# A limit on the loads in flight at the start of a fused attention and expert kernel

## The chip, the core and the metric

The kernel runs on one core of one Trainium2 chip. The metric is the device time of one execution in microseconds (us); the number that counts is the median of the runs. The profile adds one execution recorded in detail, whose span runs from the first to the last instruction.

## The reference

Three stages follow each other. What is computed, cut to what matters (the masks are a plain window of 32 positions for heads 0 to 3, and a window of 128 in steps of 4 for heads 4 to 7):

```python
# q, k, v: [2, 8, 576, 64]
scores = where(mask, q @ k.T / sqrt(64), -1e9)
attn   = softmax(scores);  x = attn @ v             # reshaped to [1152, 512]
h      = x @ w_in                                   # w_in [512, 1024], float64
solu   = h * softmax(h)
ln     = (solu - mean) / sqrt(var + 1e-6) * g_ln
x2     = ln @ w_out                                 # w_out [1024, 512], float64
for e in range(4):                                  # w1 [4, 512, 1024], w2 [4, 1024, 512]
    out += p[:, e] * (relu(x2 @ w1[e]) @ w2[e])
```

## The kernel before

Everything is written out by hand: `ORDER` (L31 to L53) is a list of steps, and each engine gets its instructions in that order. Each step takes one piece of a generator. The steps with a lower-case `l` are loads, all issued by SyncE (SP, its queue is shown as SPq) and all on one hardware queue, in the order of the list: `lP`/`lD` fetch a tile of q and k (416 or 448 KB, `load_qk`, L151), `lvp`/`lvd` a tile of v (384 KB, L159 and L154), `lI` a block of 128 rows of `w_in` (`load_in`, L203 to L212) and `lO` one of `w_out` (512 KB, `load_out`, L228). `lI.0` and `lI.4` are the two halves of block 0 of `w_in`, 512 KB each; `lI.1`, `lI.2` and `lI.3` are whole blocks of 1 MB.

SP issues 28 loads of this kind in the first 31 us, and one of 22 KB (`misc`). Their order begins

1 `lP.0.0`, 2 `lI.4`, 3 `lD.0.0`, 4 `lD.1.0`, 5 `lP.1.0`, 6 `lI.0`, 7 `lP.2.0`, 8 `lD.2.0`, 9 `lI.1`, 10 `lI.2`, 11 `lvp.0.0`, 12 `lvd.1.0`, 13 `lI.3`, 14 `lvp.1.0`, 15 `lvd.0.0`, 16 `lD.1.1`, 17 and 18 `lO.0.0` and `lO.0.1`, then `misc` and ten more tiles of q, k and v.

These numbers are used below. The program has eight completion semaphores for its DMAs and gives them out in turn, so an issue also waits until the load that had its semaphore before, eight DMAs back, has landed.

What the loads feed: `UP`/`UD` (`att_U`, L257) is one unit of attention, with the score matmuls at L275 (q and k needed), maximum, subtraction, exponent and sum on VectorE (DVE, L296 to L305) and ScalarE (ACT, L301), and the product with v at L337. `VI` (`conv_in`, L214) turns a block of float64 `w_in` into two float32r parts: ACT L190 and L192 read the raw block (`draw`), DVE L194, L196 and L198 put the bits together, L223 and L225 split the result. `conv_in` works on a whole block of 1 MB at once for blocks 1 to 3, and on a half for block 0. `H` (`moe_H`, L367) is x @ w_in on TensorE (PE); `F` is a matmul on a constant tile, without use for the result. After the front come the expert products at L562 and L634.

Of the kernel before, what the change touches and what calls it, by code (L numbers as in the profile page):

```python
# [13 lines left out]
I64 = mybir.dt.int64  # L14
# [9 lines left out]
SWAP = (3, 4, 5, 6, 7, 8)  # L24
ROWS = (5,)
EB = 4
VB = 3
EXPB = ()
ASWAP = ("UD.0.1", "UD.1.1", "UD.2.1", "UP.1.1", "UP.2.1")
# [26 lines left out]
def fused_kernel(ctx, tc, qkp, qkd, vp, vd, w_in, w_out, gp, w1, w2, out):  # L56
    nc = tc.nc
# [44 lines left out]
    xlo = wp.tile([128, KD, NT], F32R, name="xlo", tag="xlo")  # L102
    ep = lnw.enter_context(tc.tile_pool(name="ep", bufs=EB))
    cvs = ExitStack()
# [3 lines left out]
    ap2 = at.enter_context(tc.tile_pool(name="ap2", bufs=2))  # L108
    ap3 = at.enter_context(tc.tile_pool(name="ap3", bufs=VB))
    early = ExitStack()  # L110
    erp = early.enter_context(tc.tile_pool(name="erp", bufs=1, side="right"))

    qkP, qkD, vdt = [], [], []
# [31 lines left out]
    nc.gpsimd.memset(mhalf, -0.5)  # L145

    vps = {}

    def load_qk(quad, t, b):
        dst, src = ((qkD, qkd), (qkP, qkp))[quad == "P"]  # L150
        nc.sync.dma_start(out=dst[b][t], in_=src[b, t])  # L151

    def load_vd(c, b):
        nc.sync.dma_start(out=vdt[b][c].rearrange("p m h d -> p (m h d)"), in_=vd[b, c])  # L154

    def load_vp(u, b):
        t = ap3.tile([128, 3, 4, D], F32, name="vp", tag="vp")
        vps[u, b] = t
        nc.sync.dma_start(out=t.rearrange("p m h d -> p (m h d)"), in_=vp[b, u])  # L159

    whi, wlo = {}, {}
    alt = [False]
# [21 lines left out]
    cvr = cv.tile([128, 2048], I32, name="cvr", tag="cvr")  # L184
# [18 lines left out]
    def load_in(j):  # L203
        j, half = j % 4, j // 4
        if j not in dins:
            dins[j] = erp.tile([128, 2048], I32, name=f"draw{j}", tag=f"draw{j}")
        r = dins[j]
        if half:
            nc.sync.dma_start(out=r[:, 1024:2048].bitcast(I64), in_=w_in[128 * j:128 * j + 128, 512:1024])
            return  # L210
        n = 512 if j == 0 else 1024
        nc.sync.dma_start(out=r[:, 0:2 * n].bitcast(I64), in_=w_in[128 * j:128 * j + 128, 0:n])  # L212

    def conv_in(j):  # L214
        j, half = j % 4, j // 4
# [9 lines left out]
        pick().tensor_tensor(out=lo, in0=a, in1=hi.bitcast(F32), op=ALU.subtract)  # L225

    def load_out(j, t):
        nc.sync.dma_start(out=cvr[:, 1024 * t:1024 * t + 1024].bitcast(I64), in_=w_out[256 * j + 128 * t:256 * j + 128 * t + 128, :])  # L228

    def conv_out(j, t):  # L230
        sl = slice(512 * t, 512 * t + 512)
# [454 lines left out]
    def load_misc():  # L686
# [4 lines left out]
              "VI": conv_in, "VO": conv_out, "H": moe_H, "T": moe_T, "X": moe_X, "WP": prep_w1, "XQ": prep_x,  # L691
              "WV": prep_w2, "u": lambda s: up(s, 0), "d": lambda t: down(0, t)}
    single = {"lD": lambda t, b: load_qk("D", t, b), "lP": lambda t, b: load_qk("P", t, b), "lvd": load_vd, "lvp": load_vp,
              "lI": load_in, "lO": load_out, "F": warm_up,
              "misc": load_misc, "endE": end_early, "endA": end_att, "endH": end_H, "lW": load_w1, "lV": load_w2, "endX": end_X, "sc": scales}
    for name in ORDER.split():
        name, _, n = name.partition("*")
# [108 lines left out]
```

## Time and profile before

| what | value |
|---|---|
| median of 3 runs | 528.22 us |
| lowest, highest | 528.07, 528.5 us |
| the profiled execution | 528.32 us |
| its span, first to last instruction | 526.5 us |
| busy in the span: PE, DVE, ACT, POOL | 98%, 68%, 36%, 35% |
| DMA | 46.44 MB, 88 GB/s over the span |

The time of the profiled execution stands 1.8 us over its span and 0.1 us over the median. Busy shares are means over stages that differ: most bytes of the front move in the first 40 us, when DVE is also at its busiest.

### The profile page before, as it was taken

How to read it: one execution, taken by the hardware profiler on the slowest of the kernel's cores; microseconds unless marked ns; L12 is line 12 of the kernel's file. 1: busy time of each engine (PE TensorE's matmuls, PEld its weight loads, DVE VectorE, ACT ScalarE, POOL GpSimd, SP SyncE). 2: the span in 40 equal slices, each digit the busy share in tenths (PEclk: the TensorE clock that was granted, in tenths of full speed). 3: DMA queues.
4: the chain of work that ended last, by engine and by line, in shares of the span. 5: the costliest groups of instructions: out<-in, count | busy, mean ns of one | idle time of the engine just before them, and what ended most of it. 6: DMA issues, size and time to landing. Idle time of an engine off the chain costs nothing.

```text
span 526.5 us, 9419 instructions
## 1 busy us (share of the span) xinstructions
PE 513.6 (98%) x3971; PEld 457.9 (87%) x3971; DVE 356.4 (68%) x474; ACT 190.6 (36%) x294; POOL 186.7 (35%) x131
## 2 busy tenths in 40 slices
PE   7789999998999999999999999999999999999997
PEld 3568889888999999998989899898989989898986
DVE  7999898484999875754775485568448655853532
ACT  3766884363153422421422233142223213312200
POOL 3334321111345632830661273047117313820300
PEclk9999999999999999999999999999999999999999
DMA  8984462546062001300400040040005002000022
GB/s 321 409 319 149 146 202 78 143 159 200 1 225 95 1 1 50 111 1 1 159 1 1 8 153 0 2 153 7 2 0 161 1 0 81 0 1 1 1 81 100
DMA packets 24490, 46.44 MB, mean 88 GB/s; under 512 B 4480, under 2 KB 9088, under 8 KB 24064
## 3 DMA queue, kind: packets, MB, share of 16 engines
q1 hardware_dynamic: 24448, 45.84, 25.4%
q8 instruction: 31, 0.51, 0.4%
q14 instruction: 11, 0.09, 0.1%
HBM read 39.34 MB, written 6.49 MB: 87 GB/s over the span
## 4 chain that ended last, share of the span: by engine, by line
PE 90%; DMA 4%; DVE 2%; ACT 1%; issue 1%; SPq 1%; ACTq 0%
PE pa L634 19%; PE pm L634 18%; PE pm L562 17%; PE pa L562 17%; PE pm L367 9%; PE pm L449 6%; DMA draw<-in_moe_w_in_dram 2%; PE pa L337 1%; DMA dt<-st 1%; DMA et<-dt 1%; PE pa L275 1%; PE pa L398 1%; SPq L151 0%; DVE hl L436 0%; ACT eva L192 0%
## 5 line engine op out<-in xcount | busy, mean ns | idle before, releaser
L575 DVE SCALAR_TENSOR_TENSOR hl<-ct,hh 128x512 fp32r<-128x512 f32 (+1 forms) x64 | 64.1, 1018 | 32.4 <-ACT hh L573 32.4
L573 ACT ACTIVATE hh<-ct 128x512 fp32r<-128x512 f32 (+1 forms) x64 | 42.2, 682 | 50.8 <-DVE ct L605 21.3
L634 PE MATMUL pa<-wl,hh 128*128 128x512 f32 (+1 forms) x148 | 57.3, 387 | 0.0
L634 PE MATMUL pa<-wh,hh 128*128 128x512 f32 (+1 forms) x148 | 57.2, 387 | 0.0
L634 PE MATMUL pa<-wh,hl 128*128 128x512 f32 (+1 forms) x148 | 57.1, 386 | 0.0
L562 PE MATMUL pm<-xoh,hl 128*128 128x256 f32 (+1 forms) x192 | 56.8, 296 | 0.0
L562 PE MATMUL pa<-xoh,hl 128*128 128x256 f32 (+1 forms) x192 | 56.8, 296 | 0.0
L562 PE MATMUL pm<-xol,hh 128*128 128x256 f32 (+1 forms) x192 | 56.8, 296 | 0.0
L562 PE MATMUL pa<-xol,hh 128*128 128x256 f32 (+1 forms) x192 | 56.8, 296 | 0.0
L562 PE MATMUL pm<-xoh,hh 128*128 128x256 f32 (+1 forms) x192 | 56.8, 296 | 0.0
L562 PE MATMUL pa<-xoh,hh 128*128 128x256 f32 (+1 forms) x192 | 56.8, 296 | 0.0
L634 PE MATMUL pm<-wl,hh 128*128 128x512 f32 (+1 forms) x144 | 55.7, 387 | 0.0
L634 PE MATMUL pm<-wh,hh 128*128 128x512 f32 (+1 forms) x144 | 55.7, 387 | 0.0
L634 PE MATMUL pm<-wh,hl 128*128 128x512 f32 (+1 forms) x144 | 55.6, 386 | 0.0
L481 POOL TENSOR_TENSOR wl<-wl,wh 128x1024 fp32r<-128x1024 f32 x7 | 16.9, 2413 | 94.7 <-ACT wh L176 94.7
L639 DVE SCALAR_TENSOR_TENSOR xf<-pm,pr,xf 128x512 f32<-128x512 f32 (+1 forms) x32 | 23.6, 738 | 31.1 <-PE pm L634 31.1
L639 DVE SCALAR_TENSOR_TENSOR xf<-pa,pr,xf 128x512 f32<-128x512 f32 (+1 forms) x32 | 23.6, 738 | 30.3 <-PE pa L634 30.3
L589 POOL TENSOR_TENSOR ct<-ct,ct 128x512 f32<-128x512 f32 (+1 forms) x16 | 24.1, 1506 | 54.3 <-ACT ct L587 54.3
L176 ACT CAST wh<-wl 128x1024 fp32r<-128x1024 f32 x16 | 16.8, 1052 | 70.3 <-PE pa L634 39.8
L481 POOL TENSOR_TENSOR hl<-sw,hh 128x512 fp32r<-128x512 f32 x20 | 29.4, 1475 | 28.2 <-ACT hh L176 28.2
L562 PEld LDWEIGHTS pm<-xoh,hh 128*128 128x128 f32 x192 | 36.4, 190 | 0.3
L562 PEld LDWEIGHTS pm<-xol,hh 128*128 128x128 f32 x192 | 36.4, 190 | 0.3
(200 smaller groups left out, 1258.5 us busy)
## 6 DMA issues: line engine op xcount, KB each, us to landing
wl<-in_moe_w_dram SPq DMA_DIRECT2D x16, 512.0 KB, 4.3
cvr<-in_moe_w_out_dram SPq DMA_DIRECT2D x8, 512.0 KB, 3.5
rw<-in_moe_w_dram SPq DMA_DIRECT2D x8, 512.0 KB, 4.9
wh<-in_moe_w_dram SPq DMA_DIRECT2D x8, 512.0 KB, 6.5
draw<-in_moe_w_in_dram SPq DMA_DIRECT2D x3, 1024.0 KB, 11.9
qkD<-in_qkd_dram SPq DMA_DIRECT2D x6, 448.0 KB, 9.9
dt<-st SPq DMA_DIRECT2D x5, 512.0 KB, 3.0
et<-dt SPq DMA_DIRECT2D x10, 256.0 KB, 4.8
```

Of the source, the lines that this page charges most:

```text
L176: nc.scalar.copy(out, in_)
L275: nc.tensor.matmul(ps[32 * g:32 * g + 32, j, 64 * m:64 * m + 64], lhsT=qt[rows, h, xq:xq + 32], rhs=kt[rows, h, xq:xq + 64], start=False, ...
L337: nc.tensor.matmul(po[64 * (g % 2):64 * (g % 2) + 64, j, o:o + 32], lhsT=vt[rows, m, g, :], rhs=pt[rows, m, g, :], start=True, stop=True)
L367: nc.tensor.matmul(pm[:, n, :], lhsT=xx[:, kk, cols], rhs=ww["in", kk][:, 512 * n:512 * n + 512], start=(n_ == 0 and i < 2), stop=(n_ == K ...
L449: nc.tensor.matmul(pm[:, dd, 0:CW], lhsT=w_, rhs=x_[:, f, :], start=(f == 0 and i == 0), stop=(f == KF - 1 and i == 2))
L481: pick().tensor_tensor(out=out, in0=a, in1=b, op=op)
L562: nc.tensor.matmul(ps[:, ff, 0:n], lhsT=a[:, kk, fc], rhs=b[:, kk, :], start=kk == 0 and m == 0, stop=kk == 1 and m == 2)
L573: nc.scalar.activation(out=hv, in_=src, func=AF.Relu)
L575: nc.vector.scalar_tensor_tensor(out=lv, in0=src, scalar=0.0, in1=hv.bitcast(F32), op0=ALU.max, op1=ALU.subtract)
L589: poolv().tensor_tensor(out=c12, in0=c21, in1=c22, op=ALU.add)
L634: nc.tensor.matmul(po[:, 0, 0:dn], lhsT=h_[:, f, cols], rhs=w_, start=(f == 0 and i == 0), stop=(f == 3 and i == 2))
L639: nc.vector.scalar_tensor_tensor(out=acc[:, t, dc], in0=po[:, 0, 0:dn], scalar=pr[:, t, e:e + 1], in1=acc[:, t, dc], op0=ALU.mult, op1=ALU ...
```

## The change

Every load of q, k, v, `w_in` and `w_out` goes through a new helper `load`. It keeps a list of the loads issued so far with a size in KB (a nominal 432 for q and k, 384 for v, 512 for a block of weights). It goes back through that list, adds up the sizes, its own first, and makes the new load wait for the landing of the first earlier load with which the sum would pass `FLY` = 2000 KB. The wait is SP's, ahead of the issue. The loads of 1 MB become two of 512 KB; `conv_in` is as before. `misc` and the later transfers do not go through `load`.

```diff
+FLY = 2000
...
+    inq = []
+    def load(out, in_, kb):
+        i = nc.sync.dma_start(out=out, in_=in_)
+        inq.append((i, kb))
+        for p, n in reversed(inq[:-1]):
+            kb += n
+            if kb > FLY:
+                tc.add_manual_dep(i.ins, p.ins.name, mybir.DependencyInfo(mybir.DependencyClass.Sync, mybir.DependencyReason.DATA),
+                                  reason="few loads in flight")
+                break
...
     def load_qk(quad, t, b):
-        nc.sync.dma_start(out=dst[b][t], in_=src[b, t])
+        load(dst[b][t], src[b, t], 432)
...
         if half:
-            nc.sync.dma_start(out=r[:, 1024:2048].bitcast(I64), in_=w_in[128 * j:128 * j + 128, 512:1024])
+            load(r[:, 1024:2048].bitcast(I64), w_in[128 * j:128 * j + 128, 512:1024], 512)
             return
-        n = 512 if j == 0 else 1024
-        nc.sync.dma_start(out=r[:, 0:2 * n].bitcast(I64), in_=w_in[128 * j:128 * j + 128, 0:n])
+        for n in range(0, 512 if j == 0 else 1024, 512):
+            load(r[:, 2 * n:2 * n + 1024].bitcast(I64), w_in[128 * j:128 * j + 128, n:n + 512], 512)
```

`load_vd`, `load_vp` and `load_out` change in the same way (384, 384 and 512 KB).

## Rows read from the trace of the kernel before

**Rows 1.** The page: one engine's line of part 1, DMA's of part 2.

```profile
PE 513.6 (98%) x3971; PEld 457.9 (87%) x3971; DVE 356.4 (68%) x474; ACT 190.6 (36%) x294; POOL 186.7 (35%) x131
...
DMA  8984462546062001300400040040005002000022
```

**Rows 2.** The chain of waits, 0 to 135 us: start us, us, what.

```profile
4.51 11.89 DMA draw<-in_moe_w_in_dram
...
30.79 2.94 PE pm L367 x12
```

**Rows 3.** Busy time by stretch (busy us and instructions, PEclk, DMA share, GB/s).

```profile
30.80:111.60 80.80, 79.81 (x968) 67.91 (x968) 66.77 (x110) 51.56 (x83) 23.69 (x17) 1.00 0.50 162
```

**Rows 4.** Timeline of SP, 0 to 41 us: start us, us, line, what.

```profile
0.72 0.39 SPq L151 DMA_DIRECT2D qkP<-in_qkp_dram  x1
...
4.51 1.19 SPq L212 DMA_DIRECT2D draw<-in_moe_w_in_dram  x2
7.25 0.33 SPq L159 DMA_DIRECT2D vp<-in_vp_dram  x1
...
9.55 0.33 SPq L212 DMA_DIRECT2D draw<-in_moe_w_in_dram  x1
10.82 0.33 SPq L159 DMA_DIRECT2D vp<-in_vp_dram  x1
12.09 0.57 SPq L154 DMA_DIRECT2D vd<-in_vd_dram  x1
13.93 0.33 SPq L151 DMA_DIRECT2D qkD<-in_qkd_dram  x1
16.42 2.85 SPq L228 DMA_DIRECT2D cvr<-in_moe_w_out_dram  x2
...
23.40 0.33 SPq L154 DMA_DIRECT2D vd<-in_vd_dram  x1
...
25.36 0.47 SPq L151 DMA_DIRECT2D qkP<-in_qkp_dram  x1
...
29.60 1.07 SPq L151 DMA_DIRECT2D qkP<-in_qkp_dram  x2
40.78 0.33 SPq L228 DMA_DIRECT2D cvr<-in_moe_w_out_dram  x1
```

**Rows 5.** Timeline of ACT, 4 to 31 us, the raw w_in blocks.

```profile
5.14 0.67 ACT L190 ACTIVATE draw<-draw 128x512 int32<-128x512 uint32 x1 [3.14 <-DMA draw<-in_moe_w_in_dram]
...
16.42 1.16 ACT L190 ACTIVATE draw<-draw 128x1024 int32<-128x1024 uint32 x1 [0.27 <-DMA draw<-in_moe_w_in_dram]
...
20.46 1.20 ACT L190 ACTIVATE draw<-draw 128x1024 int32<-128x1024 uint32 x1
...
25.31 1.17 ACT L190 ACTIVATE draw<-draw 128x1024 int32<-128x1024 uint32 x1
```

**Rows 6.** Timeline of PE, score matmuls: load 3, and the qkP issued at 25.36.

```profile
7.28 0.97 PE L275 MATMUL pa<-qkD 64*32 64x64 f32 x48 [1.05 <-DMA qkD<-in_qkd_dram]
...
35.39 0.73 PE L275 MATMUL pa<-qkP 64*32 64x64 f32 x48
```

**Rows 7.** Busy time by stretch, all engines (columns as rows 3).

```profile
4.00:7.00 3.00, 2.23 (x53) 1.13 (x52) 2.10 (x6) 1.63 (x3) 0.00 (x0) 1.00 0.98 342
```

**Rows 8.** Issues at 0.72, 25.36, 46.70 and 48.19: KB, us to landing.

```profile
qkP<-in_qkp_dram SPq DMA_DIRECT2D x1, 416.0 KB, 3.1
...
qkP<-in_qkp_dram SPq DMA_DIRECT2D x1, 416.0 KB, 8.8
...
pt<-da SPq DMA_DIRECT2D x1, 96.0 KB, 3.3
...
vd<-in_vd_dram SPq DMA_DIRECT2D x1, 384.0 KB, 3.5
```

**Rows 9.** Busy time by stretch of DVE alone (DVE busy, PEclk, DMA share, GB/s).

```profile
4.00:16.40 12.40, 10.68 (x26) 1.00 1.02 394
16.40:30.00 13.60, 12.78 (x19) 1.00 1.02 400
```

More of the change, by code (lines that the diff above doesn't have):

```diff
@@ L147, in fused_kernel @@
     vps = {}
+    inq = []
[8 more added lines that the diff above has]
+                break
     def load_qk(quad, t, b):
         dst, src = ((qkD, qkd), (qkP, qkp))[quad == "P"]
-        nc.sync.dma_start(out=dst[b][t], in_=src[b, t])
+        load(dst[b][t], src[b, t], 432)
     def load_vd(c, b):
-        nc.sync.dma_start(out=vdt[b][c].rearrange("p m h d -> p (m h d)"), in_=vd[b, c])
+        load(vdt[b][c].rearrange("p m h d -> p (m h d)"), vd[b, c], 384)
     def load_vp(u, b):
@@ L158, in load_vp @@
         vps[u, b] = t
-        nc.sync.dma_start(out=t.rearrange("p m h d -> p (m h d)"), in_=vp[b, u])
+        load(t.rearrange("p m h d -> p (m h d)"), vp[b, u], 384)
     whi, wlo = {}, {}
@@ L227, in load_out @@
     def load_out(j, t):
-        nc.sync.dma_start(out=cvr[:, 1024 * t:1024 * t + 1024].bitcast(I64), in_=w_out[256 * j + 128 * t:256 * j + 128 * t + 128, :])
+        load(cvr[:, 1024 * t:1024 * t + 1024].bitcast(I64), w_out[256 * j + 128 * t:256 * j + 128 * t + 128, :], 512)
     def conv_out(j, t):
```

## Prediction

> **What bounds the kernel now.** I read the page first: TensorE (PE) is busy for 98% of the span, and the DMA engines are near full only in the first slices of 13 us [rows 1]. So a change to the first loads can move the end in one way: by moving the moment from which PE is fed without a break. The chain of waits shows where that is. It runs through the landing of `draw`, block 1 of w_in, issued at 4.51 us and landed 11.89 us later, at 16.40; from there through ScalarE (ACT) and VectorE (DVE) work; from 30.79 us on it is nearly all PE [rows 2]. In the stretch from 30.8 to 111.6 us PE is busy for 79.81 of 80.80 us [rows 3]. A us that the front gains or loses before 30.8 is thus about a us of the whole; one behind that is hidden as long as no load comes later than its reader.
>
> Next the timeline of SP, which tells how loads land [rows 4]. Ten loads are issued by 5.7 us, and from then on each issue stands at the landing of the load eight before it. Load 11 goes out at 7.25, where load 3 has just let PE go on at 7.28 [rows 4, 6]; load 17 goes out at 16.42, where load 9 has just let ACT go on [rows 4, 5]. Read so, the start of each issue is the landing of an earlier load: load 5 at 9.55, load 6 (512 KB) at 10.82, load 7 at 12.09, load 8 at 13.93, load 9 (1 MB) at 16.42, load 10 (1 MB) at 16.42 + 2.85 - 0.33 = 18.94, load 13 (1 MB) at 23.40. They land in the order of issue, one at a time: 1.27 us for 512 KB, 2.49 and 2.52 us for 1 MB, about 410 KB per us. The long times to landing (8.8 us for a q and k tile [rows 8]) are time in line. The line is in order, so its length does not set when a load lands; what stands ahead of it in bytes does.
>
> **The change part by part.** *The limit.* Going through the list, loads 1 to 4 wait for nothing; load 5 waits for load 1, 6 for 2, 7 for 3, 8 for 4, the halves of block 1 (new numbers 9 and 10) for loads 5 and 6, those of block 2 (11 and 12) for 7 and 9, and from there on nearly each load waits for the one four before it. This replaces the present wait for the one eight before. The halves of block 1 are issued at about 9.6 and 10.9 us in place of 4.51. That costs nothing if the DMA engines still have work when the new load reaches them. Work ahead: usually three loads are in flight at the moment of release, the smallest such three (two of 384 KB and one of 416 KB) 1184 KB, at 410 KB per us 2.9 us; at load 12 only two, 1024 KB, 2.5 us. Time to bridge, from issue to landing without the transfer: the first load of 416 KB takes 3.1 us, 1.0 of them transfer, so 2.1; a lone load of 384 KB at 48.19 takes 3.5, so 2.6; a small one of 96 KB takes 3.3, so 3.1 [rows 8]. The loads of the change are like the first two, so I take 2.1 to 2.6, with 3.1 as the upper end. At 2.6 there is a gap of 0.1 us at load 12 and none elsewhere. At 3.1 there is one of 0.6 us at load 12 and of 0.2 us at the tightest rounds after it. Load 12 is half of block 2, which landed at 18.94 and is read at 20.46 [rows 4, 5]: 1.5 us of cover. Block 3 landed at 23.40 and is read at 25.31: 1.9 us. The q and k tile issued at 25.36 lands 8.8 us later, at 34.2, and is read at 35.39 [rows 4, 6, 8]: 1.2 us, the thinnest of these. Term of the limit: 0; upper end by these rows 0.2.
>
> *The halves.* 2 x 1.27 against 2.49 or 2.52 us: 0.05 us later for block 1, which has no cover (ACT sat idle for 0.27 us before it [rows 5]), and 0.02 us each for blocks 2 and 3, which have. `conv_in` still reads the whole block, so the earlier half gains nothing. Term: +0.05. A rule of the Trainium skill speaks against this part: "DMA: Bandwidth & Descriptors", section Rules for kernel authors, wants at least 1 MiB in each DMA for the highest bandwidth. The same page (section Measured) puts a lone 1 MB at 78% of the peak, so by it I would expect halves to lose more than that; the intervals in the line do not bear this out, 512 KB moves at the pace of 1 MB.
>
> *SP's own work.* Three more issues of about 0.4 us, and the waits. Behind them on SP stand only further loads. Load 30 of the new list waits until about 35 us, where the last issue of the burst now ends at 30.7; SP's next issue is at 40.78 and waits for a buffer [rows 4]. Cover of some 5 us, term 0; without it the next w_out block would start late by what is over.
>
> Sum against the profiled execution: 528.32 + 0 + 0.05 + 0 = 528.37. That execution is 0.1 over the median of the runs, so 528.3 for the median.
>
> **The rivals.** *Slower: the line runs dry.* If under load the time to bridge is much more than a lone load shows, each round of four loads loses (bridge - 3.2 us), 3.2 being three mean loads of some 1300 KB. Up to the second half of block 1 there are one and a half rounds. A bridge of 4.5 us makes block 1 land 2.0 us late, with ACT waiting for it: 528.3 + 2.0 = 530.3. It decides from 3.9 us on (1.5 x 0.7 = 1.06 us, the 0.2% bound). For it: the line hides the bridge of each load after the first, so no row shows it under load. Against: the three loads that do show it give 2.1 to 3.1. The Trainium skill, the same page, section Latency and other measured facts, has HBM access latency at 0.2 us on average and 2 us at high load, and calls it the main part of a DMA's fixed cost; by that an estimate of 2.6 + 1.8 = 4.4 us would be in reach, and no row here tells.
>
> *Faster: a shorter line moves better.* From 4 to 7 us the engines are busy for a share of 0.98 and move 342 GB/s, where 394 is the mean to 16.4 us [rows 7, 9]. By the landings load 3 (448 KB, from 5.14 to 7.25) takes 2.1 us, load 8 (448 KB, 12.09 to 13.93) 1.84, where 1.1 is the pace [rows 4, 5]: 1.7 us lost on the way to block 1. Should these stalls come from ten issues being pushed in at once, they go, and the loads land up to 1.7 us earlier. But DVE is idle for only 12.40 - 10.68 = 1.7 us between 4 and 16.4 us and for 0.8 us from there to 30 [rows 9], and the gaps are not all waits for loads. About half of the 1.7 is what I would expect then: 527.4; all of it: 526.6. For it: the stalls stand in the time of the densest issues. Against: between 7.25 and 12.09 the line is as long and the pace is nearly full.
>
> *Nothing that can be measured, for another reason:* the eight semaphores hold SP back already, so that only depth changes and all landings stay. That is my forecast itself; a wait that did not take effect would give the same time, 528.2.
>
> **How the numbers follow.** A change of 0.2%, 1.06 us, is about what a measurement of this kernel can tell from none. Forecast, landings stay: 0.58, its own range 527.2 to 529.4. The line runs dry: 0.24, 529.3 to 531 and over. A shorter line moves better: 0.18, most of it between 526.4 and 527.2; half gains below 0.2% belong to the forecast. The predicted time is 528.3. The range goes from 526.7 to 530.6; I leave about 0.07 below and 0.1 above. Faster 0.18, same 0.58, slower 0.24.
>
> **What would show it.** In the profile after: block 1's halves issued near 9.6 and 10.9 us, ACT's first read of the whole block near 16.4, that of block 2 near 20.5 and of block 3 near 25.3; DMA share still about 1.0 in all stretches from 4 to 36 us; PE's first stretch without gaps from about 30.8. A DMA share of 0.9 or less between 7 and 31 us, and ACT waiting longer than 0.27 us for block 1, would be the line running dry. GB/s over 390 between 4 and 7 us, and the read of block 1 before 16, would be the shorter line. The prediction is wrong if block 1 lands more than 1 us away from 16.4, or if with all landings in place the work behind 31 us falls in another order.

## The result and the profile after

The changed kernel is slower: 531.98 us median (530.07 to 533.07, 5 runs) against 528.22 (527.93 to 529.04, 5 runs), a ratio of 1.0066 with a 95% interval of 1.0040 to 1.0091. The prediction was 528.3, with a range of 526.7 to 530.6: the time lies above the range, and on the side that had a chance of 0.24. The profiled execution took 532.77 us, with a span of 531.0. Lines move by 12 behind the new helper: L275 is now L287, L367 L379, L190 L202; every front load is issued at L152.

The page of the kernel after, PE's line of part 1 and two lines of part 2 (in tenths, 40 slices of 13.3 us):

```profile
PE 515.9 (97%) x3971; PEld 459.4 (87%) x3971; DVE 356.7 (67%) x474; ACT 190.8 (36%) x294; POOL 187.1 (35%) x131
...
PEclk9988999999999999999999999999999999999999
DMA  8995563545153000500400040031004002000022
```

Busy work is what it was [rows 1]; the 4.5 us that the span has gained are time in which PE waits or runs slower, in the front. SP's timeline has 27 loads and `misc` in the first 31 us before the change (28 DMAs in all, nine tiles behind `misc`; the section on the kernel before gives one more of each), and 30 loads in all in the kernel after. The timeline after shows them going out one by one:

```profile
3.92 0.33 SPq L152 DMA_DIRECT2D qkP<-in_qkp_dram  x1
...
7.61 0.33 SPq L152 DMA_DIRECT2D qkP<-in_qkp_dram  x1
...
9.77 6.16 SPq L152 DMA_DIRECT2D draw<-in_moe_w_in_dram  x4
...
17.78 0.33 SPq L152 DMA_DIRECT2D vd<-in_vd_dram  x1
19.39 1.61 SPq L152 DMA_DIRECT2D draw<-in_moe_w_in_dram  x2
...
26.45 1.99 SPq L152 DMA_DIRECT2D cvr<-in_moe_w_out_dram  x2
...
35.06 0.33 SPq L152 DMA_DIRECT2D qkP<-in_qkp_dram  x1
```

Each start is again the landing of an earlier load, now usually the fourth before. Load 5 goes out at 3.92, when load 1 has landed, and so on: the tile of v at 17.78 waits for load 10, the second half of block 1; the second of the two issues from 19.39 (19.39 + 1.61 - 0.33 = 20.67) waits for load 12, the second half of block 2; the first at 26.45 for load 16, the second half of block 3. Against the landings before [rows 4]:

| what | landed before | after | later by |
|---|---|---|---|
| block 1 | 16.42 | 17.78 | 1.4 us |
| block 2 | 18.94 | 20.67 | 1.7 us |
| block 3 | 23.40 | 26.45 | 3.1 us |
| the P tile of q and k issued at 25.36 before, 35.06 now | 34.2 | 39.3 | 5.1 us |

The line no longer moves at its pace. Busy time by stretch, first of the kernel before, then after (busy us and instructions of PE, PEld, DVE, ACT, POOL, then PEclk, DMA share, GB/s):

```profile
7.00:16.40 9.40, 8.98 (x262) 5.23 (x262) 8.59 (x21) 3.20 (x6) 4.26 (x5) 1.00 1.03 411
16.40:36.00 19.60, 16.17 (x389) 11.84 (x388) 18.72 (x29) 15.75 (x24) 4.85 (x4) 1.00 1.02 399
```

```profile
4.00:7.00 3.00, 2.22 (x53) 1.12 (x52) 2.05 (x6) 1.63 (x3) 0.00 (x0) 1.00 0.95 312
...
7.00:16.40 9.40, 8.76 (x262) 5.21 (x262) 8.51 (x20) 3.20 (x6) 4.06 (x4) 1.00 0.97 346
16.40:36.00 19.60, 15.47 (x291) 11.36 (x290) 17.50 (x28) 13.94 (x21) 4.92 (x5) 0.91 0.93 320
```

Read the last two columns together. The share falls only from 1.03 to 0.97 and 0.93, but the rate falls from 411 and 399 to 346 and 320 GB/s. Whoever looks for idle DMA engines finds almost none: the packets stay in the engines longer for the same bytes.

What waits for it, first in ACT's timeline after (the reads of blocks 1, 2 and 3, then of the first w_out block):

```profile
17.85 1.15 ACT L202 ACTIVATE draw<-draw 128x1024 int32<-128x1024 uint32 x1 [1.49 <-DMA draw<-in_moe_w_in_dram]
...
21.84 1.18 ACT L202 ACTIVATE draw<-draw 128x1024 int32<-128x1024 uint32 x1
...
26.68 1.20 ACT L202 ACTIVATE draw<-draw 128x1024 int32<-128x1024 uint32 x1
...
35.06 0.70 ACT L202 ACTIVATE cvr<-cvr 128x512 int32<-128x512 uint32 x1 [2.81 <-DMA cvr<-in_moe_w_out_dram]
```

Block 1 is waited for 1.49 us where it was 0.27 [rows 5], and ACT is 1.4 us late from there. Blocks 2 and 3 then come late too, but ACT, late itself, does not wait for them. The timeline of PE shows the second and larger wait, and a third cost. First before, then after:

```profile
34.47 0.72 PE L275 MATMUL pa<-qkD 64*32 64x64 f32 x48
...
38.97 0.67 PE L337 MATMUL pa<-pt,vd 64*64 64x32 f32 x31 [0.87 <-issue]
...
39.84 0.73 PE L275 MATMUL pa<-qkD 64*32 64x64 f32 x48
```

```profile
36.32 0.72 PE L287 MATMUL pa<-qkD 64*32 64x64 f32 x48
...
39.38 0.84 PE L287 MATMUL pa<-qkP 64*32 64x64 f32 x48 [2.06 <-DMA qkP<-in_qkp_dram]
40.15 1.22 PE L379 MATMUL pm<-wh,xhi 128*128 128x512 f32 x2
41.17 1.05 PE L379 MATMUL pm<-wl,xhi 128*128 128x512 f32 x2
...
44.11 0.72 PE L287 MATMUL pa<-qkD 64*32 64x64 f32 x48
...
45.34 0.63 PE L379 MATMUL pm<-wl,xhi 128*128 128x512 f32 x2
```

The score matmuls on the D tile ahead start 1.9 us late (36.32 against 34.47), those on the P tile 4.0 us (39.38 against 35.39 [rows 6]): the wait for the P tile makes 2.1 us of it. Then pairs of matmuls that take 0.63 us at 45 take 1.05 us at 41. That costs more, but the stop of 0.87 us at 38.97 before is not there after, and by the next D tile PE is 4.3 us late (44.11 against 39.84). Two stretches of the kernel after (columns as above) show the clock behind the longer matmuls:

```profile
26.00:29.00 3.00, 3.00 (x27) 1.97 (x27) 3.00 (x6) 2.52 (x6) 0.83 (x1) 0.50 0.97 303
...
40.00:42.90 2.90, 2.90 (x21) 1.82 (x6) 2.48 (x6) 1.58 (x3) 0.47 (x1) 0.50 0.98 357
```

The granted clock is 0.50 there, the level of 1.2 GHz; the profiled execution before had 1.00 in all its front. Ahead of the second of these stretches PE had waited 2.06 us for the tile. The low level is not the change's alone, though: of 59 executions of the kernel before that stood beside the experiments, 27 had a mean granted clock below 0.999 (mean time 529.2 us, against 528.4 us for the other 32); of the changed kernel all five had (0.994 to 0.997). So a part of the loss goes with the clock, and these times do not tell how much.

### The profile page after: what moved, and what is told of

Its sections match the earlier page's. It is cut to its first block, busy times and chain, and to the rows that moved or that the text cites. A ratio compares the mean times of both kernels' runs of the same rounds, so it can differ in the third digit from the quotient of the medians.

```text
span 531.0 us, 9422 instructions
## 1 busy us (share of the span) xinstructions
PE 515.9 (97%) x3971; PEld 459.4 (87%) x3971; DVE 356.7 (67%) x474; ACT 190.8 (36%) x294; POOL 187.1 (35%) x131
## 4 chain that ended last, share of the span: by engine, by line
PE 88%; DMA 9%; DVE 1%; SPq 0%; issue 0%; ACT 0%; DVEq 0%; ACTq 0%
PE pa L646 19%; PE pm L646 18%; PE pm L574 17%; PE pa L574 17%; PE pm L379 9%; PE pm L461 6%; DMA qkP<-in_qkp_dram 3%; DMA vp<-in_vp_dram 2%; DMA cvr<-in_moe_w_out_dram 1%; PE pa L349 1%; DMA draw<-in_moe_w_in_dram 1%; DMA dt<-st 1%; DMA et<-dt 1%; PE pa L287 1%; PE pa L410 1%; DVE hl L448 0%
```

## The experiments

Each kernel was run in five rounds beside the kernel before, which had medians of 528.48 us (the first four), 528.59 (the next four) and 528.68 (the last two).

| kernel | median us | ratio to before, 95% interval |
|---|---|---|
| halves alone | 528.69 | 1.0021, 1.0009 to 1.0033 |
| limit alone, whole blocks | 533.12 | 1.0100, 1.0077 to 1.0122 |
| limit of 4000 KB | 528.57 | 1.0007, 0.9990 to 1.0024 |
| limit of 3000 KB | 529.40 | 1.0023, 1.0012 to 1.0034 |
| limit on the first 16 loads | 531.97 | 1.0070, 1.0044 to 1.0096 |
| limit from load 17 on | 529.83 | 1.0019, 1.0002 to 1.0036 |
| the P tile two places earlier | 532.07 | 1.0057, 1.0032 to 1.0081 |
| halves by rows, limit of 2000 KB | 549.30 | 1.0376, 1.0351 to 1.0402 |
| halves by columns, limit of 2000 KB | 533.31 | 1.0066, 1.0043 to 1.0090 |
| limit of 1200 KB | 546.38 | 1.0326, 1.0301 to 1.0352 |

**Halves alone.**

```diff
-FLY = 2000
+FLY = 100000
```

> The limit is out of reach (100000 KB), the w_in blocks still come as halves. Theory A (the limit makes the line in front of the DMA engines too short, so that they lose time at the start of each load): the loss is gone, 528.2 us, within 0.7 us, and the P tile of q and k that TensorE waited for at 39.3 us lands near 34 again. Theory B (the halves cost, more and smaller loads): the loss stays, about 532 us.

528.69 us: most of the loss is gone (0.2 us stays by the medians; by the ratio 0.2% or 1.1 us, over the 0.7 us allowed). The P tile, issued at 26.85, lands within 8.0 us, by 34.9, and the profile moves 395 and 400 GB/s in the two stretches from 7 and from 16.4 us. Theory A. What the halves cost is between nothing and 1.1 us: the kernel with 4000 KB below has them too, at a ratio of 1.0007 with 1 inside its interval.

**Limit alone.** The 1 MB loads stay whole, at 1024 KB each in the sum.

```diff
-        for n in range(0, 512 if j == 0 else 1024, 512):
-            load(r[:, 2 * n:2 * n + 1024].bitcast(I64), w_in[128 * j:128 * j + 128, n:n + 512], 512)
+        n = 512 if j == 0 else 1024
+        load(r[:, 0:2 * n].bitcast(I64), w_in[128 * j:128 * j + 128, 0:n], n)
```

> The limit of 2000 KB stays, the w_in blocks come whole, 1024 KB each. Theory A (line too short): at least as slow as the changed kernel, 532 us or more, since two blocks of 1 MB can't be in flight together and the line is at its shortest around them. Theory B (the halves cost): back at 528.2 us.

533.12 us, Theory A again. Here block 2 waits for block 1 alone, and the line does run empty. The stretch behind it:

```profile
16.40:20.00 3.60, 2.19 (x10) 0.86 (x9) 2.91 (x7) 2.50 (x4) 2.17 (x3) 1.00 0.33 84
```

A share of 0.33 at 84 GB/s is what an empty line looks like; the changed kernel's 0.93 at 320 GB/s is something else.

**The size of the limit.**

```diff
-FLY = 2000
+FLY = 4000        # and 3000, and 1200, in kernels of their own
```

> Halves and a limit of 4000 KB, so each load waits for the one eight or nine before it, with the extra waits still there. Theory A (line too short): 528.2 us, within 0.7 us. Theory C (the extra waits and their handling on SP's queue cost by themselves): near 532 us, as with 2000 KB.

> Halves and a limit of 3000 KB, about six loads in flight. Theory A (line too short): between, 528.2 to 530 us, since two more loads ahead are 2.2 us more of work than with 2000 KB. Theory C (waits cost by themselves): near 532 us.

> A limit of 1200 KB, two loads in flight. Theory A (line too short): the loss grows faster than in proportion, since with two loads the line is empty for part of every round: a round of two loads takes the bridge of 2.1 to 2.6 us and one transfer of 1.1, 3.2 to 3.7 us for 2.2 us of transfers, so the 30 loads take 15 to 22 us longer and the end comes 12 to 20 us later, 540 to 548 us.

528.57, 529.40 and 546.38 us, each in the range that Theory A gave. With 4000 KB each wait is for the load eight or nine before, which the eight semaphores ask for anyway, so it shows only that waits already met cost nothing. The run that decides against Theory C is the one with 3000 KB: there most waits are for the load six before, so they do hold SP back, and yet the pace is full and the ratio no higher than with the halves alone (1.0023 and 1.0021). The two stretches with 3000 KB, and with 1200 KB:

```profile
7.00:16.40 9.40, 8.27 (x259) 5.22 (x262) 8.48 (x20) 3.23 (x7) 4.05 (x4) 1.00 1.03 403
16.40:36.00 19.60, 16.71 (x392) 12.02 (x391) 19.09 (x31) 15.75 (x24) 5.08 (x5) 1.00 1.03 400
```

```profile
7.00:16.40 9.40, 6.66 (x155) 3.47 (x156) 6.09 (x14) 2.16 (x5) 2.05 (x2) 1.00 0.69 220
16.40:36.00 19.60, 13.82 (x229) 9.24 (x227) 13.38 (x24) 9.91 (x16) 4.51 (x5) 0.74 0.70 224
```

403 and 400 GB/s with 3000 KB, 346 and 320 with 2000, 220 and 224 with 1200: the full pace needs a limit between 2000 and 3000 KB here. From these rates follows an estimate of the time to bridge under load, which the kernel before could not show. With 1200 KB about 900 KB are in flight (two loads); at 222 GB/s, 217 KB per us, a round of two takes 4.1 us, less one transfer of 1.1 us is 3.0. With 2000 KB about 1800 KB are in flight; at 333 GB/s, 325 KB per us, a round takes 5.5 us, and the bridge is 4.4 us.

The estimate takes the time that a load is in flight to be one round, so it holds whatever a load spends behind the others, and it is not one fixed time: 3.0 with two loads, 4.4 with four. With nothing ahead the time is short. In the kernel with the limit alone, block 2 went out when block 1 had landed, and block 3 when block 2 had:

```profile
17.91 0.33 SPq L152 DMA_DIRECT2D draw<-in_moe_w_in_dram  x1
...
22.64 0.33 SPq L152 DMA_DIRECT2D draw<-in_moe_w_in_dram  x1
```

That is 4.7 us for 1 MB, 2.5 of them transfer [rows 4], which leaves 2.2 us; lone loads had shown 2.1 to 3.1 [rows 8]. The lone loads were read rightly, then, but the time did not stay at 2.2 with other loads in flight.

**Where in the list it costs.** The limit on a part of the loads only.

```diff
-            if kb > FLY:
+            if kb > FLY and len(inq) <= 16:        # the other kernel: len(inq) > 16
```

> The limit of 2000 KB for the first 16 loads only (to the end of w_in); from there on only the eight semaphores hold SP back. Theory D (a load that lands late costs what is over its cover; the profile of the change lands block 3 of w_in 3.0 us late and the P tile of q and k that TensorE waited for 5.2 us late, cover 1.2): what is lost on the first 16 stays lost, since the line is full after them, so the tile lands about 3.0 us late and the end is 3.0 - 1.2 = 1.8 us later, 530.0 us. Theory E (only the stretch behind 31 us matters, where the tile is waited for): 528.3.

> The limit for loads 17 and later only. Theory D: the tile is late by the rest, 5.2 - 3.0 = 2.2 us, the end by 2.2 - 1.2 = 1.0 us, 529.3 us; w_in lands as without a limit. Theory E: all of the loss is here, about 532.

531.97 and 529.83 us. Theory E falls: the first 16 loads alone make the whole loss. The later ones alone make about 1 us, so the two do not add up. The second kernel is near Theory D's 529.3, the first is 2 us over D's 530.0, and its profile shows what D left out. The P tile lands at 37.4 (issued at 29.45, 7.9 us), 3.2 us late as D has it, but PE does not wait for it: PE is 2.1 us late by 34.3 already, behind the late w_in blocks and tiles of v. D's 1.8 us is close to that by luck. The rest is two waits in PE's timeline with the limit on the first 16 loads:

```profile
36.24 0.39 PE L379 MATMUL pm<-wh,xlo 128*128 128x512 f32 x1 [0.63 <-issue]
...
42.59 0.67 PE L349 MATMUL pa<-pt,vd 64*64 64x32 f32 x31 [1.89 <-issue]
```

These two waits are for nothing that the profile shows; before, PE waited 0.87 us at the second place and hardly at the first (0.12 us). PE stops there behind the same matmul, the 17th of its group, in four profiles: before (0.87 us), here (1.89), with the limit from load 17 on (1.14) and with the P tile earlier (1.01). In each the q8 queue, which moves instructions, had begun to move a block of 16 KB 2.2 to 3.1 us before PE went on (here between 40.00 and 40.25 us), and likewise 2.5 to 2.7 us before the end of the wait at 36.24. That PE waited for its own instructions is likely; it is argued, not shown, and why the wait is longer here stays open. With the limit from load 17 on, the profile has a stretch at the low level of the clock, in rows by stretch and in PE's timeline:

```profile
41.50:44.80 3.30, 3.30 (x8) 2.54 (x9) 1.86 (x3) 0.22 (x1) 0.58 (x1) 0.50 0.43 161
```

```profile
39.80 0.66 PE L349 MATMUL pa<-pt,vd 64*64 64x32 f32 x31 [1.14 <-issue]
...
42.25 1.05 PE L379 MATMUL pm<-wl,xhi 128*128 128x512 f32 x2
...
45.77 0.62 PE L379 MATMUL pm<-wh,xhi 128*128 128x512 f32 x2
```

That execution took 531.67 us. The times of this kernel's twelve runs go from 528.26 to 531.67: three with a mean clock of 0.999 or more took 528.26, 528.80 and 529.82 us, nine at 0.994 to 0.997 took 528.63 to 531.67. The longer times go with the low level, but it does not set them alone. Nor did each such wait go with a fall: the profile with the limit on the first 16 loads has the longest of these stops, 1.89 us, and a mean clock of 1.000.

**The tile that PE waited for.**

```diff
-lD.0.1+ lvd.2.0+ UP.2.0+ UD.1.1+ UD.0.0 VO.0.1 VI.2+ lvp.0.1 lP.0.1
+lD.0.1+ lP.0.1 lvd.2.0+ UP.2.0+ UD.1.1+ UD.0.0 VO.0.1 VI.2+ lvp.0.1
```

> The changed kernel with its limit, but the P tile of q and k that TensorE waited for at 39.3 us is loaded two places earlier, ahead of two tiles of v (768 KB, 1.9 us at the full pace) that are read later. Theory D (TensorE's wait for this load sets the end): about 1.9 us comes back, 530.0 us. Theory F (the end is set by w_in's late blocks and the wait for the tile only absorbs it): 531.5 to 532, nothing comes back.

532.07 us: nothing that can be told came back (ratios of 1.0057 and 1.0066, each with an interval of some 0.25% to either side), as Theory F has it. The 1.9 us of Theory D would be 0.36%, at the edge of what such intervals can exclude. PE's timeline:

```profile
29.45 0.90 PE L349 MATMUL pa<-pt,vp 64*64 64x32 f32 x48 [2.18 <-DMA vp<-in_vp_dram]
...
32.15 1.05 PE L379 MATMUL pm<-wl,xhi 128*128 128x512 f32 x2
...
39.44 0.73 PE L287 MATMUL pa<-qkP 64*32 64x64 f32 x48
```

PE no longer waits for the P tile: it has landed by 36.44, when SP issues a load that waits for it, 2.9 us earlier than in the changed kernel. Yet PE reads it at 39.44, where it was 39.38. A late tile of v (2.18 us) and a stretch at the low clock behind it stand in its place, beside the late w_in blocks that F names (the first pairs of x @ w_in begin at 25.63, 24.41 before). That tile of v is load 17, ahead of the place of the edit; it landed at 29.3 here and at 28.1 in the profile after, where PE read it at 28.50. So about 1 us of the difference is one between two executions, and the pair of profiles does not show what the tile's wait was worth by itself. The chain of waits names the wait that came last; ahead of it, other late loads were ready to take its role.

**Bytes or number of loads.** Each load is cut in two, by rows or by columns, so that the same KB are in flight in twice as many loads.

```diff
     def load(out, in_, kb):
+        for p in (0, 64):
+            load_part(out[p:p + 64], in_[p:p + 64], kb / 2)
+    # the other kernel: n = in_.shape[1] // 2, then out[:, c:c + n], in_[:, c:c + n] for c in (0, n)
+    def load_part(out, in_, kb):
```

> The limit of 2000 KB stays, but each load is cut in two by partitions (64 rows each), so the same KB are in flight in twice as many loads. If the bytes in flight set the pace: as slow as the changed kernel or slower (twice as many loads to start), 532 us or more. If the number of loads in flight sets it: back towards 528.5.

> The limit of 2000 KB stays and each load is cut in two by columns, all 128 rows in each, so the same KB are in flight in twice as many loads, with rows half as long. If the bytes in flight set the pace: as slow as the changed kernel or slower, 532 us or more. If the number of loads in flight sets it: back towards 528.5, as with 4000 KB.

549.30 us by rows, 533.31 by columns. By rows the question is not answered, since these loads to 64 partitions are slow with the engines full:

```profile
7.00:16.40 9.40, 6.17 (x155) 3.38 (x155) 5.52 (x12) 3.75 (x6) 2.05 (x2) 1.00 1.05 230
```

230 GB/s throughout, with a share of 1.05. By columns:

```profile
7.00:16.40 9.40, 5.78 (x153) 3.25 (x154) 6.16 (x14) 5.18 (x8) 2.06 (x2) 1.00 1.03 379
16.40:36.00 19.60, 18.01 (x392) 12.54 (x391) 18.69 (x32) 14.72 (x22) 6.75 (x6) 0.91 1.00 340
```

Doubling the number of loads does not bring the time back, which speaks for bytes. It is not clean either: rows are half as long, and the loss is spread otherwise (the first stretch at 379 GB/s, and PE and DVE busy for less of it).

No version beat the kernel before; 4000 KB is level with it.

## Why the prediction was wrong, step by step

**What bounds the kernel, and where a late load goes:** right. The loss was made before 45 us (4.3 us at 44.11) and stayed to the end: x @ w_in ends at 116.0 on the chain of waits where it was 111.6, and the span is 4.5 us longer.

**"Term of the limit: 0":** this is the step that failed. It held that the length of the line "does not set when a load lands", kept the pace at about 410 KB per us, and compared the work ahead, 2.5 to 2.9 us, with a bridge of 2.1 to 2.6 us taken from loads in a nearly empty line (the "lone" one at 48.19 had two of 96 KB ahead of it). With four loads in flight the pace was 346 and 320 GB/s where it had been 411 and 399, block 1 landed 1.4 us late, block 3 3.1 and the P tile 5.1, and the median rose by 3.8 us. Put as a bridge, this is about 4.4 us, by the estimate from the rates. The text said that no row showed the bridge under load, and still let the lone loads decide.

The rival "the line runs dry" had the direction and, with its 4.5 us, nearly the size; that engines stand idle between rounds is not what the shares of 0.97 and 0.93 show. It had block 1 late by 2.0 us, measured 1.4; its price of 530.3 was too small because it stopped at block 1. What came behind cost more: a tile 5.1 us late with a wait of 2.06 us, and stretches at half the clock. The range ended at 530.6 for that reason.

On the Trainium skill: "DMA: Bandwidth & Descriptors", section Latency and other measured facts, with its HBM latency of 0.2 us on average and 2 us at high load, pointed the right way. The prediction's estimate of 4.4 us from it is also what the rates with 2000 KB give, but with 1200 KB they give 3.0, so the match is in part luck. No run shows that HBM is where the time goes.

**The covers:** 1.5, 1.9 and 1.2 us were read rightly, but used as if each load had its own for good. A reader that is late itself gives the loads behind it more cover (block 3 was 3.1 us late and still ready when ACT came 1.4 us late). And when one wait is taken away, the next late load takes its place, as the P tile showed.

**The halves, +0.05 us:** small, as said; by the run with the limit out of reach 0.2 (medians) or 1.1 us (ratio), by the one with 4000 KB 0.1 or 0.4 us.

**SP's own work, 0:** right, by the run with 3000 KB, where waits hold SP back and the pace is full. Its cover was used up, though: the last load of the burst went out at 40.76, not at about 35. The next `w_out` load, at 40.78 before, went out at 44.74, and that wait is again one for a buffer (put down to POOL), late like all the rest.

**"A shorter line moves better":** wrong. From 4 to 7 us the rate was 342 GB/s before [rows 7] and 312 after, with fewer issues in that time; with the limit out of reach, and as many issues as before, it was 291. So the number of issues does not set it; what slows this first stretch is open.

**What would show it:** ACT's wait for block 1 and its time (1.49 us, 17.85) did. The DMA share of 0.9 or less did not as clearly (0.97 and 0.93): the marker should have been the rate.

**Open:** why packets stay longer in the engines when the line is short. The runs show that it depends on how much is in flight; they do not part KB from the number of loads cleanly, nor show which part of a load's way takes the time. What the low clock costs of the loss is open too.

## What to carry to other kernels

A load's place in an ordered line tells when it lands only as long as the line is deep enough for the time from issue to landing under load; that time can't be taken from a load that ran alone (here 2.2 us, against an estimate of 4.4 with four in flight), so a limit is tried at two or three depths before one is kept. Judge DMA engines by GB/s and share together: a line that was somewhat too short showed as a share of 0.93 at 320 GB/s, not as idle engines; only with 1200 KB did the share fall to 0.69, at 220 GB/s. Once several loads are late, the wait named by the chain is only the last of them, and mending it alone may bring nothing.

## What the runs showed of the hardware that was not expected

- Limit on the KB in flight against rate, from 7 to 36 us, loads of 384 to 512 KB on one queue: 220 to 224 GB/s with 1200 KB, 320 to 346 with 2000, 400 to 403 with 3000, 400 with 4000, and 395 to 400 with the eight semaphores alone (399 to 411 in the kernel before, with three loads of 1 MB).
- Loads to 64 partitions moved at 230 GB/s with a share of 1.05, against about 400 for 128 partitions. The Trainium skill's page "SBUF — State Buffer", section "Can I just issue two DMAs to hit both halves?", says that two such halves serialize; the run agrees with it.
- The granted clock fell to 0.50 (1.2 GHz) in the front of the changed kernel, from 26 to 29 us and from 40 to 42.9 us, the second time behind a wait of PE of 2.06 us. A pair of matmuls took 1.05 us there and 0.63 us later. In the kernel with the halves alone it averaged 0.72 from 25 to 31 us with the loads at full pace (396 GB/s).
